# Convolution stages re-ordered behind the FFN's evictions, a fused gate, and rows that are centred but not divided

## The chip, the cores and the metric

The kernel runs on one core of a Trainium2 chip. A core has TensorE (PE; its weight loads are listed apart as PEld), VectorE (DVE), ScalarE (ACT), GpSimd (POOL) and SyncE (SP), each with an in-order queue of its own, and 16 DMA engines that move what the queues of SP, ACT and POOL issue. Times are microseconds (us) on the device. The kernel before took 1149.67 us, the median of 3 runs (1146.87 to 1152.59); the profiled execution took 1154.33.

## The reference

x is 2048 rows of 576, the output has the same shape. Two branches read the normalized rows xn and are added to x:

```python
xn = (x - mean(x)) / sqrt(var(x) + 1e-5)              # per row
# branch A: short causal convolution, product, long convolution, gate
k_shift[s] = sum over t < 4 of k[s - t] * shift_k[:, t]
kv = k_shift * v
y  = irfft(rfft(pad(kv)) * rfft(pad(ssm_k)))[:2048] + kv * ssm_D   # per channel
A  = xn * y
# branch B
B  = relu(xn @ w1) @ w2                                # 576 -> 4608 -> 576
out = x + A + B
```

All is float32. A product is made exact enough by splitting each operand into a rounded high part and the rest (hi, lo) and adding hi*hi, hi*lo and lo*hi.

## The kernel before

**FFN.** The 2048 rows are 16 tiles t of 128 rows, four blocks b of four tiles (BT = 4), two halves of two blocks. For each half, all 12 chunks of 384 hidden units pass over its two blocks. `mm1` (L276) makes one 128x512 block of hidden units in 14 matmuls; ACT's L281 takes relu into hh, DVE's L282 the rest into ll. `mm2` (L296) makes one 128x288 half of an output tile in 9 matmuls; DVE adds it to acc[t] (L299), which began as x. The weights of a chunk are loaded by SP (L234 to L243) and split by ACT (L251, L259) and POOL (L224). `make_xT` computes a block's mean and deviation (`stats`, `inv_std`), normalizes (L181), transposes on PE (L214) and splits into xhi, xlo, xhl. For block 0 this stands at the kernel's start; `make_xT` for the second half is traced in the first half's last chunk.

**Convolution.** The long convolution is a transform of length 2048 with a shift of a quarter bin, so that the product of transforms is the causal convolution's; it is written as 64 x 32, in four stages of a generator `conv`. fk: the table ssm_k (kt, 4.7 MB in packets of 128 bytes, L339) is split (`stack`, L320 on ACT and L321 on DVE) and transformed (`first`, L327) to zk in DRAM. fx: for each tile, the four taps of the short convolution and the product with v (L397 to L405, on DVE), split, transformed to zx. fm, the middle stage, 32 groups: the second step of both transforms (L455), their complex product on ACT and DVE (L471 to L499), the first step back, to zy. fo, the last stage, 16 tiles: the second step back (L537, L539), assembled from PSUM (L541 on ACT, L542 on DVE), gated with the normalized rows (L181, then L549), and added to the FFN's result: for t < 8, whose FFN result was stored to DRAM as fin, on POOL (L553) and stored; for t >= 8 into acc[t] (L556), before the FFN stores it.

**What sets the order.** Every seventh matmul of `mm1` (3,584 columns) and every ninth of `mm2` (2,592 columns) calls `tick` with its columns. A tick credits the convolution `rate` times the columns; when its credit is not negative it runs the generator to the next `yield`. `yield W` costs W of credit; `yield -PAUSE` lets that many FFN columns pass first. That gives the order in which operations are traced. It is not yet the queues' order: a planner (the tile framework's timeline scheduler) then orders each engine's queue by its own estimate of when operands are ready and buffers free, with the traced order as priority. `tc.issue_after(ins)` makes the operations traced within it stand behind `ins` in the queue of ins's engine. How far the planner moves operations shows in the trace: the statistics of the second half's rows (L166 on xn), traced in the twelfth chunk, run at 67 us.

PSUM: two tiles for mm1, three for mm2, three for the convolution and the transposes.

Of the kernel before, what the change touches and what calls it, by code (L numbers as in the profile page):

```python
# [17 lines left out]
P = 128  # L18
# [27 lines left out]
PAUSE = 20000  # L46
START = 40000
PAUSES = 7.5
SHARE = 0.93
# [3 lines left out]
W_FK, W_FX, W_FM, W_FO = 1.6, 4.4, 2.0, 2.8  # L53
KD = 72
# [52 lines left out]
def h3_ffn_kernel(ctx: ExitStack, tc, x, k, v, shift_k, ssm_k, ssm_D, w1, w2, fwd, inv, mid, out):  # L107
# [39 lines left out]
    def move(tile_, rows, t, store=False):  # L147
        for u in range(U):
            a, b = tile_[halves(u)[0]], rows[u, :, t]
            nc.sync.dma_start(*((b, a) if store else (a, b)))  # L150
# [3 lines left out]
    def load_x(t, tag, bufs):  # L154
        pair = xp.tile([P, 2, D], F32, tag=tag, name=f"{tag}{t}", bufs=bufs)
        move(pair, x, slice(t, t + 2))
        return pair

    def load_acc(t):
        pairs[t] = load_x(t, "acc", HT // 2)  # L160
        acc[t], acc[t + 1] = pairs[t][:, 0, :], pairs[t][:, 1, :]
# [21 lines left out]

    xT = {}
    done = {}

    def make_xT(b, srcs, in_place=False):

# [3 lines left out]
        xT[b] = (hi, lo, hl)  # L192
        t0 = b * BT
        with tc.issue_after(done["dve"].ins) if done else nullcontext():
            for t in range(t0, t0 + BT):
                stats(t, srcs[t])
            inv_std(t0, BT)
        xn = []
        for t in range(t0, t0 + BT):
# [6 lines left out]
            normalized(xn[-1], srcs[t], t)  # L206
        for c in range(5):
            w = min(P, D - c * P)
            if b == 0 and c >= 3:
                ps = ps_o.tile([P, 512], F32, tag="o", name=f"psx{c}")  # L210
            else:
                ps = fft_psum()
            for i in range(BT):
                nc.tensor.transpose(ps[:w, i * P:(i + 1) * P], xn[i][:, c * P:c * P + w], ident)  # L214
            if c < 4:
                nc.scalar.activation(hi[:, c, :], ps, AF.Copy)
                nc.vector.tensor_tensor(lo[:, c, :], ps, hi[:, c, :], OP.subtract)  # L217
            else:
                done["act"] = nc.scalar.activation(hl[:64, :], ps[:64, :], AF.Copy)
                done["dve"] = nc.vector.tensor_tensor(hl[64:, :], ps[:64, :], hl[:64, :],  # L220
                                                      OP.subtract)
# [63 lines left out]
    def mm2(ci, b, i):  # L285
        t = b * BT + i
        cols = slice(i * P, (i + 1) * P)
        for h in range(2):
# [10 lines left out]
            nc.vector.tensor_tensor(acc[t][:, dc], ps[:, :NH], acc[t][:, dc], OP.add)  # L299
            tick(W_MM2 / 2)  # L300
        if ci % NCHUNK == NCHUNK - 1:
            if t < HT:
# [26 lines left out]

    def conv():  # L330

        with tc.tile_pool(name="fk", bufs=2) as fp:
            kt = fp.tile([P, NH, A2], F32, tag="kt", name="kt", bufs=1)
            for d in range(0, NH, KD):
# [3 lines left out]
            skip = fp.tile([P, NH], F32, tag="skip", name="skip", bufs=1)  # L340
            for h in range(2):
                nc.sync.dma_start(skip[h * A1:h * A1 + 1, :], ssm_D[None, h * NH:(h + 1) * NH])
            yield -2 * PAUSE
            for h in range(2):
                row = slice(h * A1, h * A1 + 1)
                nc.vector.tensor_tensor(kt[row, :, 0], kt[row, :, 0], skip[row, :], OP.add)

            def prepare(t):
                stk = fp.tile([P, 2, NH], F32R, tag="stk", name=f"ks{t}")
                for h in range(2):  # L350
                    stack(stk[:, h, :], kt[:, :, t], h)
                return stk

            order = [T * u + t for t in range(T) for u in range(U)]
# [4 lines left out]
            nxt = prepare(order[0])  # L359
            yield -PAUSE / 2  # L360
            for n, t2 in enumerate(order):
                stk = nxt
                u, t = divmod(t2, T)
                z = fp.tile([P, D], F32, tag="z", name=f"zk{t2}")
                for h in range(2):
                    first(ws[t], stk[:, h, :], z[:, h * NH:(h + 1) * NH], u)
                    if h == 0 and n + 1 < len(order):
                        nxt = prepare(order[n + 1])
# [6 lines left out]
        with tc.tile_pool(name="fx", bufs=2) as fp:  # L375
# [3 lines left out]
            win = {}  # L379

            def load_k(t):
                win[t] = fp.tile([P, D], F32, tag="k", name=f"k{t}", bufs=KS + 1)
                if t >= 0:
                    move(win[t], k, t)
                else:
# [4 lines left out]
            def prepare(t):  # L390
                if t + 1 < T:
                    load_k(t + 1)
                w = load_const(fp, fwd[t], f"wx{t}")
                vt = fp.tile([P, D], F32, tag="v", name=f"v{t}")
                move(vt, v, t)
                c = fp.tile([P, D], F32, tag="c", name=f"c{t}", bufs=2)
                nc.vector.tensor_tensor(c, win[t], sk[:, 0, :], OP.mult)  # L397
                for n in range(1, KS):
                    e = fp.tile([P, D], F32, tag="e", name=f"e{t}_{n}", bufs=2)
                    nc.vector.tensor_tensor(e, win[t - n], sk[:, n, :], OP.mult)  # L400
                    nc.vector.tensor_tensor(c, c, e, OP.add)  # L401
                return w, vt, c

            def finish(w, vt, c, t):
                nc.vector.tensor_tensor(c, c, vt, OP.mult)  # L405
                stk = fp.tile([P, U, D], F32R, tag="stk", name=f"xs{t}")
                for u in range(U):
                    stack(stk[:, u, :], c, u)
                return w, stk

            for t in range(1 - KS, 1):
                load_k(t)
            pre = prepare(0)
            ready = finish(*pre, 0)
            pre = prepare(1)
            yield -PAUSE
            for t in range(T):
                w, stk = ready
                for u in range(U):
                    z = fp.tile([P, D], F32, tag="z", name=f"zx_{t}_{u}")  # L420
                    for h in range(2):
                        cols = slice(h * NH, (h + 1) * NH)
                        first(w, stk[:, u, cols], z[:, cols], u)
                        if h == 0 and u == 0 and t + 1 < T:
                            ready = finish(*pre, t + 1)
                        yield W_FX
                    nc.sync.dma_start(zx[:, T * u + t, :], z)
                if t + 2 < T:
                    pre = prepare(t + 2)
            yield -PAUSE  # L430


        with tc.tile_pool(name="fm", bufs=2) as fp:
# [6 lines left out]
            def second(z, g, name):  # L440
                zt = fp.tile([P, D], F32, tag="zt", name=f"zt{name}", bufs=3)
                nc.sync.dma_start(zt, rows(z, g))
                hi = fp.tile([P, D], F32R, tag="hi", name=f"hi{name}", bufs=4)
                lo = fp.tile([P, D], F32R, tag="lo", name=f"lo{name}", bufs=4)
                nc.scalar.activation(hi, zt, AF.Copy)
                nc.vector.tensor_tensor(lo, zt, hi, OP.subtract)
                return hi, lo
# [10 lines left out]
            def both(g):  # L458
                return second(zk, g, f"k{g}"), second(zx, g, f"x{g}")

            pend = None
            nxt = both(0)
            yield -PAUSE
            for g in range(NG + 1):
                if g < NG:
                    (kh, kl), (xh, xl) = nxt
                    k1 = fp.tile([P, D], F32, tag="k1", name=f"k1_{g}")
                    k2 = fp.tile([P, D], F32, tag="k2", name=f"k2_{g}")
                    for h in range(2):
                        ps, cols = run(kh, kl, 0, h)  # L470
# [4 lines left out]
                        yield W_FM  # L475
# [202 lines left out]
```

## Time and profile before

| | before |
|---|---|
| median of 3 runs | 1149.67 us (1146.87 to 1152.59) |
| profiled execution | 1154.33 us |
| its span | 1152.5 us |
| mean granted PE clock | 0.977 |
| PE busy | 1095.9 us (95%) |
| DVE, ACT, POOL busy | 707.0, 584.5, 266.4 us |
| moved by DMA | 150.78 MB, 131 GB/s |
| matmuls of fk, fx, fm, fo | 128, 128, 576, 128 of 6534 |

Busy time counts an engine as busy while any of its instructions runs; idle time is put down to what released the engine. The granted clock is the share of PE's full clock; a matmul takes longer where it is below 1. Stretches of the trace are read with PE's busy time and clock side by side, since a wait of PE can be followed by a stretch at a lower clock.

### The profile page before, as it was taken

To read this page: it belongs to the slowest core of one execution; us is meant where nothing else is said; L and a number is where in the kernel's file an instruction comes from. 1 tells how busy PE (TensorE), PEld (TensorE's weight loads), DVE (VectorE), ACT (ScalarE), POOL (GpSimd) and SP (SyncE) were. 2 spreads that over 40 slices of the span, in tenths; PEclk is the share of its full clock that TensorE was granted. 3 is DMA by queue.
4 is the path that set the end of the run, shared out by engine and by line. 5 is a ranking of instruction groups with operands and counts; after the bars stand their busy time and mean duration, and the time that the engine had idled before them with its cause. 6 is when DMAs were issued, how large, how long until landed. Compare 5 with 4: busy or idle time off the path is not lost.

```text
span 1152.5 us, 17373 instructions
## 1 busy us (share of the span) xinstructions
PE 1095.9 (95%) x6534; PEld 990.5 (86%) x6534; DVE 707.0 (61%) x1223; ACT 584.5 (51%) x1178; POOL 266.4 (23%) x207
## 2 busy tenths in 40 slices
PE   7989999899899999999999999999999998886998
PEld 4879899778799899999889899999999997775997
DVE  6367673999976733554665555555555446679832
ACT  3248783344233333566467676666767644344410
POOL 3132313133143123112121220311302213241110
PEclk8989999999999999999999999999999998997999
DMA  9955546465344234333652442333424217676203
GB/s 197 157 142 192 180 148 205 128 192 177 102 146 150 67 115 157 85 95 127 198 165 63 127 128 62 128 96 98 123 65 135 76 33 226 197 223 176 69 1 83
DMA packets 112768, 150.78 MB, mean 131 GB/s; under 512 B 44845, under 2 KB 62895, under 8 KB 112684
## 3 DMA queue, kind: packets, MB, share of 16 engines
q1 hardware_dynamic: 105628, 138.93, 43.2%
q0 software_dynamic: 7056, 10.75, 3.8%
q8 instruction: 51, 0.84, 0.3%
q14 instruction: 33, 0.27, 0.1%
HBM read 114.26 MB, written 35.39 MB: 130 GB/s over the span
## 4 chain that ended last, share of the span: by engine, by line
PE 66%; DVE 11%; DMA 9%; SPq 5%; ACT 4%; issue 3%; POOL 1%; DVEq 0%; ACTq 0%; POOLq 0%
PE pso L296 29%; PE psh L276 29%; PE psf L455 6%; DMA r<-in_w 4%; SPq L339 3%; PE psf L327 2%; DMA xt<-in_x 2%; DVE c L401 2%; DVE e L400 2%; DVE olo L519 1%; DVE acc L299 1%; DMA kt<-in_ssm_k 1%; DVE xs L321 1%; DVE y L542 1%; SPq L234 1%
## 5 line engine op out<-in xcount | busy, mean ns | idle before, releaser
L224 POOL TENSOR_TENSOR l<-r,h 128x640 fp32r<-128x640 f32 (+1 forms) x144 | 227.8, 1596 | 643.3 <-ACT h L259 432.2
L296 PE MATMUL pso<-h,hh 128*128 128x288 f32 x1152 | 340.8, 298 | 12.1 <-DVE acc L299 11.9
L296 PE MATMUL pso<-h,ll 128*128 128x288 f32 x1152 | 340.9, 298 | 4.7 <-DVE ll L282 4.7
L296 PE MATMUL pso<-l,hh 128*128 128x288 f32 x1152 | 340.6, 297 | 0.0
L296 PEld LDWEIGHTS pso<-h,hh 128*128 128x128 f32 x1152 | 218.3, 190 | 21.8 <-DVE acc L299 15.1
L276 PE MATMUL psh<-xhi,h 128*128 128x512 f32 x576 | 228.9, 399 | 4.2 <-DVE ll L282 4.1
L276 PE MATMUL psh<-xlo,h 128*128 128x512 f32 x576 | 228.8, 397 | 0.0
L276 PE MATMUL psh<-xhi,l 128*128 128x512 f32 x576 | 227.9, 396 | 0.0
L296 PEld LDWEIGHTS pso<-l,hh 128*128 128x128 f32 x1152 | 218.7, 190 | 6.0
L296 PEld LDWEIGHTS pso<-h,ll 128*128 128x128 f32 x1152 | 218.5, 190 | 5.5 <-DVE ll L282 5.0
L299 DVE TENSOR_TENSOR acc<-pso,acc 128x288 f32<-128x288 f32 x384 | 169.4, 452 | 78.3 <-PE pso L296 76.1
L282 DVE SCALAR_TENSOR_TENSOR ll<-psh,hh 128x512 fp32r<-128x512 f32 x144 | 98.6, 687 | 130.1 <-ACT hh L281 129.5
L281 ACT ACTIVATE hh<-psh 128x512 fp32r<-128x512 f32 x144 | 85.3, 595 | 159.1 <-PE psh L276 131.1
L276 PEld LDWEIGHTS psh<-xhi,h 128*128 128x128 f32 x576 | 109.6, 191 | 22.9 <-DVE ll L282 5.7
L276 PEld LDWEIGHTS psh<-xhi,l 128*128 128x128 f32 x576 | 109.9, 191 | 20.8
L276 PEld LDWEIGHTS psh<-xlo,h 128*128 128x128 f32 x576 | 109.9, 191 | 16.7 <-DVE xlo L217 0.2
L251 ACT ACTIVATE h<-r 128x640 fp32r<-128x640 f32 x72 | 52.4, 736 | 74.7 <-DMA r<-in_w 46.9
L492 DVE TENSOR_TENSOR k<-psf,k 128x288 f32<-128x288 f32 x64 | 29.2, 456 | 74.3 <-ACT sw L491 66.8
L259 ACT ACTIVATE h<-r 128x576 fp32r<-128x576 f32 x72 | 46.6, 680 | 53.1 <-DMA r<-in_w 39.2
L490 ACT ACTIVATE sw<-psf 64x288 f32<-64x288 f32 x64 | 26.2, 409 | 67.5 <-PE psf L455 66.8
L276 PE MATMUL psh<-xhl,h 128*128 128x512 f32 x144 | 56.8, 395 | 1.1 <-DVE xhl L220 1.1
L321 DVE TENSOR_TENSOR ks<-kt,ks 64x288 fp32r<-64x288 f32 x64 | 46.6, 731 | 16.9 <-ACT ks L320 15.1
(100 smaller groups left out, 1417.3 us busy)
## 6 DMA issues: line engine op xcount, KB each, us to landing
r<-in_w SPq DMA_DIRECT2D x24, 864.0 KB, 4.9
r<-in_w SPq DMA_DIRECT2D x23, 768.0 KB, 6.0
zk<-zk SPq DMA_DIRECT2D x32, 288.0 KB, 2.5
zx<-zx SPq DMA_DIRECT2D x32, 288.0 KB, 3.2
ztk<-zk SPq DMA_DIRECT2D x32, 288.0 KB, 2.8
ztx<-zx SPq DMA_DIRECT2D x32, 288.0 KB, 2.8
zy<-vo SPq DMA_DIRECT2D x32, 288.0 KB, 2.1
zo<-zy SPq DMA_DIRECT2D x16, 576.0 KB, 6.1
```

The source lines that it names most:

```text
L224: return nc.gpsimd.tensor_tensor(dst, src, hi, OP.subtract)
L251: nc.scalar.activation(h1, r1[:, :, cols], AF.Copy)
L259: nc.scalar.activation(h2, r2[:, j, :], AF.Copy)
L276: nc.tensor.matmul(ps, a, m, start=i == 0, stop=i == len(seq) - 1)
L281: done["act"] = nc.scalar.activation(hh, ps, AF.Relu)
L282: nc.vector.scalar_tensor_tensor(ll, ps, 0.0, hh, op0=OP.max, op1=OP.subtract)
L296: nc.tensor.matmul(ps[:, :NH], a[:, cols], m[:, dc], start=n == 0, stop=n == 3 * FT - 1)
L299: nc.vector.tensor_tensor(acc[t][:, dc], ps[:, :NH], acc[t][:, dc], OP.add)
L321: nc.vector.tensor_tensor(dst[other], src[own], dst[own], OP.subtract)
L339: nc.sync.dma_start(kt[halves(h)[0], d:d + KD, :], src)
L455: nc.tensor.matmul(ps[:, :NH], a, m[:, cols], start=n == 0, stop=n == 2)
L492: nc.vector.tensor_tensor(k1[:, cols], ps, k1[:, cols], OP.mult)
```

## The change

Three things change.

**Order of the convolution.** `here()` puts an operation of the convolution on DVE behind the FFN's last traced addition (`done["acc"]`) and one on ACT behind the last traced relu (`done["act"]`). In every stage the loads, the splits and the arithmetic are taken apart and traced in small pieces between yields, loads first: kt in 16 pieces with a pause after each; x rows, matrices and z one to three steps ahead of their use, with more buffers; the short convolution tap by tap, two tiles ahead. The constants of the pacing change with it.

**Rows.** `make_xT` subtracts the mean only (`centred`). As relu and both products are homogeneous in a row's scale, 1/deviation is applied where the second product's sum is added to acc (`scalar_tensor_tensor`, same line count on DVE). `first_xT` is a new path for block 0: each tile is centred as its mean is ready, by ACT (even tiles, with the negative mean as bias) or DVE (odd), and transposed; the deviations follow. Its x rows are loaded through the queues of SP and ACT, ahead of the warm-up's other work.

**Gate.** L181, L549 and L553 or L556 become two fused DVE operations: (x - mean) * y, then that * 1/deviation + the FFN's result. The finished tiles t < 8 are stored through POOL's queue. `rest_of_stream` runs out the convolution before the last chunk's rows t >= 8 are stored.

```diff
-PAUSE = 20000
-START = 40000
-PAUSES = 7.5
-SHARE = 0.93
+PAUSE = 16000
+START = 4000
+PAUSES = 16
+SHARE = 0.95
...
-W_FK, W_FX, W_FM, W_FO = 1.6, 4.4, 2.0, 2.8
-KD = 72
+W_FK, W_FX, W_FM, W_FO = 1.6, 3.7, 1.8, 2.1
+KD = 36
+KT_GAP = 6000
...
+    def centred(dst, src, t):
+        return nc.vector.tensor_scalar(dst, src, mv[:, t, 0:1], None, op0=OP.subtract)
...
+    def first_xT(srcs):
...
+        for t in range(BT):
...
+            with tc.issue_after(behind.ins) if behind else nullcontext():
+                stats(t, srcs[t])
+                if t % 2 == 0:
+                    behind = nc.vector.tensor_scalar(neg[:, t:t + 1], mv[:, t, 0:1], -1.0, None,
+                                                     op0=OP.mult)
+                    nc.scalar.activation(xn, srcs[t], AF.Identity, bias=neg[:, t:t + 1])
+                else:
+                    behind = centred(xn, srcs[t], t)
+            for c in range(5):
+                w = min(P, D - c * P)
+                nc.tensor.transpose(ps[c][:w, t * P:(t + 1) * P], xn[:, c * P:c * P + w], ident)
+        for c in range(5):
+            split_x(0, c, ps[c])
+        with tc.issue_after(done["dve"].ins):
+            inv_std(0, BT)
...
-            normalized(xn[-1], srcs[t], t)
+            centred(xn[-1], srcs[t], t)
...
-            nc.vector.tensor_tensor(acc[t][:, dc], ps[:, :NH], acc[t][:, dc], OP.add)
+            done["acc"] = nc.vector.scalar_tensor_tensor(
+                acc[t][:, dc], ps[:, :NH], rstd[:, t:t + 1], acc[t][:, dc],
+                op0=OP.mult, op1=OP.add)
...
+            if t >= HT:
+                rest_of_stream()
...
+    @contextmanager
+    def here():
+        with tc.issue_after(done["acc"].ins), tc.issue_after(done["act"].ins):
+            yield
...
+                    yield -KT_GAP
...
-            yield -2 * PAUSE
+            yield -PAUSE
             for h in range(2):
                 row = slice(h * A1, h * A1 + 1)
-                nc.vector.tensor_tensor(kt[row, :, 0], kt[row, :, 0], skip[row, :], OP.add)
+                with here():
+                    nc.vector.tensor_tensor(kt[row, :, 0], kt[row, :, 0], skip[row, :], OP.add)
...
+            def tap(t, n):
...
+                with here():
...
+                        e = fp.tile([P, D], F32, tag="e", name=f"e{t}_{n}", bufs=1)
+                        nc.vector.tensor_tensor(e, win[t - n], sk[:, n, :], OP.mult)
+                        nc.vector.tensor_tensor(sums[t], sums[t], e, OP.add)
...
+                side = (((gate, t + 1),), ((split, t + 1, 0),),
+                        ((split, t + 1, 1),), ((tap, t + 2, 0),),
+                        ((tap, t + 2, 1),), (),
+                        ((tap, t + 2, 2),), ((tap, t + 2, 3),))
...
+                        for part in range(2):
+                            for what, *args in side[4 * u + 2 * h + part]:
+                                what(*args)
+                            yield W_FX / 2
...
+            def gate(t):
+                if t >= 0:
+                    with here():
+                        nc.vector.scalar_tensor_tensor(ys[t], rest[t][1], mv[:, t, 0:1], ys[t],
+                                                       op0=OP.subtract, op1=OP.mult)
+            def add(t):
+                if t >= 0:
+                    to, more = (ys[t], rest[t][2]) if t < HT else (acc[t], acc[t])
+                    with here():
+                        nc.vector.scalar_tensor_tensor(to, ys[t], rstd[:, t:t + 1], more,
+                                                       op0=OP.mult, op1=OP.add)
+                    if t < HT:
+                        move(to, out, t, store=True, queues=(nc.gpsimd, nc.gpsimd))
...
+                    if h == 0:
+                        if n + 1 < len(units):
+                            split(*units[n + 1])
+                        if n + 3 < len(units):
+                            load_z(*units[n + 3])
+                    else:
+                        (gate if u == 0 else add)(t - 1)
+                        if u == 0:
+                            load_rest(t + 2)
+                    yield W_FO
...
+    for t in range(0, BT, 2):
+        load_acc(t, queues=(nc.sync, nc.scalar))
+    load_w1(0)
+    load_w2(0)
...
-    make_xT(0, acc)
+    first_xT(acc)
```

In fm the diff does the same with `load` and `split` per tensor, two groups ahead, and moves the sum of the complex product and its split (L495, L498, L499) into the next group's first two steps.

More of the change, by code (lines that the diff above doesn't have):

```diff
@@ L648, in h3_ffn_kernel @@
     drain(BT)
-    for _ in stream:
-        pass
+    rest_of_stream()
 def kernel(**inputs):
```

343 lines of the change are left out of this document (187 added, 156 removed).

## The prediction

> **What bounds the kernel now.** First the page's busy times and the core's clock:
>
> ```profile
> PE 1095.9 (95%) x6534; PEld 990.5 (86%) x6534; DVE 707.0 (61%) x1223; ACT 584.5 (51%) x1178; POOL 266.4 (23%) x207
> ```
>
> ```profile
> core 0: 1152.5 us, clock 0.977
> ```
>
> TensorE bounds it: no other engine is busy for more than 61%. But 5% is not all that can be won. Busy time at the granted clock is 1095.9 x 0.977 = 1070.7 us of full-speed work, so 1152.5 - 1070.7 = 81.8 us go to waits and to the slow clock after them. The matmuls stay the same in number, so this is the most that the change can win. The view by stretches shows where it lies (columns: stretch, width, busy time of PE, weight loads, DVE, ACT, POOL, then clock, DMA share, GB/s):
>
> ```profile
> 0.00:20.00 20.00, 12.97 (x44) 7.00 (x44) 10.73 (x25) 5.16 (x9) 5.49 (x9) 0.84 0.99 228
> 50.00:70.00 20.00, 15.28 (x67) 12.81 (x66) 8.76 (x20) 5.51 (x9) 3.16 (x2) 0.83 1.18 206
> 185.00:217.00 32.00, 29.44 (x166) 26.47 (x165) 17.61 (x31) 5.73 (x10) 4.26 (x4) 0.95 0.55 152
> 217.00:300.00 83.00, 75.32 (x432) 66.43 (x432) 82.25 (x113) 32.15 (x62) 25.37 (x18) 0.98 0.54 162
> 300.00:390.00 90.00, 87.41 (x532) 79.45 (x531) 72.64 (x110) 31.34 (x60) 24.55 (x18) 1.00 0.44 132
> 545.00:605.00 60.00, 56.56 (x353) 51.71 (x353) 39.69 (x79) 34.97 (x75) 11.51 (x8) 0.97 0.62 178
> 945.00:1065.00 120.00, 99.57 (x520) 85.52 (x520) 85.03 (x144) 52.85 (x105) 37.50 (x34) 0.89 0.69 200
> 1020.00:1050.00 30.00, 21.15 (x95) 16.75 (x94) 25.61 (x42) 15.54 (x32) 13.29 (x11) 0.85 0.79 225
> 245.40:248.00 2.60, 0.36 (x3) 0.03 (x1) 2.57 (x4) 0.00 (x0) 2.05 (x2) 1.00 0.52 176
> 249.00:252.50 3.50, 3.50 (x16) 3.40 (x16) 3.47 (x7) 1.01 (x2) 0.00 (x0) 0.52 0.07 21
> ```
>
> Width less PE busy x clock is the loss of a row: 9.1 us at the start, 7.3 around 60 us, 4.0 + 9.2 + 2.6 = 15.8 in the x transform (fx), 5.1 where the second half's rows come in, 31.4 in the last stage (fo). That is 68.7 of the 81.8; the rest is thin, or the tail.
>
> What such a loss is made of stands in the chain of waits (start, length, what), then in DVE's and PE's timelines around 60 us:
>
> ```profile
> 49.10 11.44 DMA kt<-in_ssm_k
> 63.91 5.27 PE psh L276 x14
> 69.18 2.38 PE pso L296 x18
> 71.56 3.20 PE psh L276 x14
> ```
>
> ```profile
> 49.81 0.46 DVE L299 TENSOR_TENSOR acc<-pso,acc 128x288 f32<-128x288 f32 x1 [0.36 <-PE pso L296]
> 60.65 1.40 DVE L346 TENSOR_TENSOR kt<-kt,skip 1x288 f32<-1x288 f32 x2 [10.38 <-DMA kt<-in_ssm_k]
> 62.08 0.69 DVE L282 SCALAR_TENSOR_TENSOR ll<-psh,hh 128x512 fp32r<-128x512 f32 x1
> ```
>
> ```profile
> 62.82 0.61 PE L296 MATMUL pso<-h,ll 128*128 128x288 f32 x1 [4.72 <-DVE ll L282]
> ```
>
> The convolution's addition L346 stands at the head of DVE's queue until its load lands at 60.5; the FFN's own L282 is queued behind it, and PE waits for L282. Then 14 matmuls take 5.27 us where 3.20 is the full-speed price: the wait is paid twice. In fo the view of waits shows the same figure (total us, times, longest), and DVE's timeline at fx's entrance too:
>
> ```profile
> DVE xt L181 <- DMA xt<-in_x: 22.2, 10, 4.4
> PEld psf L537 <- DVE y L542: 21.6, 23, 2.8
> ```
>
> ```profile
> 203.03 0.76 DVE L400 TENSOR_TENSOR e<-k-1_1956,sk 128x576 f32<-128x576 f32 x1 [9.72 <-DMA k-1_1956<-in_k]
> ```
>
> L181 waits for x rows, the evictions L542 stand behind it, and PE waits for the PSUM they free. What costs PE is DVE's in-order queue with load-fed operations too early in it.
>
> **The slow clock.** The last two stretches above are a wait and what follows it: some 2.2 us without a matmul, then 3.5 us at clock 0.52, 1.7 us more. [...]
>
> **The start.** Rows of the timelines of DVE, PE and ACT:
>
> ```profile
> 8.54 1.54 DVE L166 BATCH_NORM_STATS2 bn<-acc 128x6 f32<-128x288 f32 x4 [0.73 <-DMA acc<-in_x]
> ...
> 12.59 4.32 DVE L181 TENSOR_SCALAR xn<-acc,mv,rstd 128x576 f32<-128x576 f32 x4
> ```
>
> ```profile
> 14.37 0.87 PE L214 MATMUL psf<-ident,xn 128*128 128x128 f32 x3 [5.52 <-DVE xn L181]
> ...
> 19.28 1.22 PE L276 MATMUL psh<-xhi,h 128*128 128x512 f32 x2
> ```
>
> ```profile
> 18.63 1.57 ACT L216 ACTIVATE xhi<-psf 128x512 fp32r<-128x512 f32 x3 [5.72 <-PE psf L214]
> ```
>
> Now the statistics of all four tiles and the whole deviation chain (to 12.59) precede the first centring. The change centres a tile as soon as its mean is there, two tiles on DVE and two on ACT, transposes tile by tile, and puts the deviation behind. The last rows still land near 8.5: the DMA share is 0.99, so a second issuing queue moves them little. From there: statistics of two tiles, 1.9 us; one centring, 1.1 (4.32 / 4); five transposes of 0.29, 1.5; one copy to xhi, 0.6. That is 13.6 against 19.28, a little earlier where DVE and ACT overlap, a us later where ACT must first split weights. I take a gain of **6** (3 to 7).
>
> **The kernel's table (kt).** Eight loads become 16 halves, and by the count of ticks L346 moves to about 200,000 of the FFN's columns, some 90 us of its work (0.45 ns a column, from 3.20 us for 7,168 and 2.38 for 5,184), where the same bytes, landed at 60.5 now, are long there. Gone: the wait of 4.7 and about 2.8 of slow clock. Kept as risk: the same bytes still pass through SP's queue ahead of the second chunk's w2, which the FFN now wants 6 us sooner. Gain **6** (2 to 7.5).
>
> **The x transform.** Groups by line on DVE (busy us, mean ns, idle before), then the tile c (ns: least, median, most):
>
> ```profile
> L299 DVE TENSOR_TENSOR acc<-pso,acc 128x288 f32<-128x288 f32 x384 | 169.4, 452 | 78.3 <-PE pso L296 76.1
> L282 DVE SCALAR_TENSOR_TENSOR ll<-psh,hh 128x512 fp32r<-128x512 f32 x144 | 98.6, 687 | 130.1 <-ACT hh L281 129.5
> L321 DVE TENSOR_TENSOR ks<-kt,ks 64x288 fp32r<-64x288 f32 x64 | 46.6, 731 | 16.9 <-ACT ks L320 15.1
> L401 DVE TENSOR_TENSOR c<-c,e 128x576 f32<-128x576 f32 x48 | 44.1, 922 | 0.3
> ```
>
> ```profile
> L401 DVE TENSOR_TENSOR c<-c,e x48: 740/751/2402, 207.0 to 393.0; 128x576 f32<-128x576 f32 x48
> ```
>
> DVE's work is the same: per t eight products and sums at 0.92 and two splits at 0.73, 8.8 us. What changes is place. Each tap goes behind the FFN's last traced evictions, about one per tick, and 16,000 columns (7.2 us) lie between loads and first tap, so most of the 9.7 us wait goes. Counting ticks by the new constants (819.2 of price over 0.95 x 2,027,520 - 256,000 - 4,000 columns is 1.48 credited per mean tick of 3,017 columns, and what the pauses saved up is spent here), a t lasts 25,300 columns: 11.45 us of FFN and 8 matmuls of 0.13, 12.5 us. In it DVE has 8.8 + 4.8 x 0.452 + 1.8 x 0.687 = 12.2 by mean durations, which count the overlap of neighbours twice: near 90%, at most 98. The stage becomes orderly but not loose. From 217 to 300, with DVE 99% full, PE lost 11%; from 300 to 390, 81% full, 3%. Between these over 200 us, 6 to 22 us; I take 9, nearer the looser row, against 15.8: gain **7** (-6 to 10).
>
> **The last stage.** Its rows on the tile xt:
>
> ```profile
> L181 DVE TENSOR_SCALAR xt<-xt,mv,rstd x16: 564/580/1625, 957.6 to 1083.2; 128x576 f32<-128x576 f32 x16
> L549 DVE TENSOR_TENSOR y<-y,xt x16: 740/742/1144, 976.7 to 1089.9; 128x576 f32<-128x576 f32 x16
> ```
>
> Removed per t: L181 and its load wait, L549, and L556 on DVE or an addition on POOL. Added: two fused operations. The trace has no such operation on SBUF alone; 0.58 and 0.74 bound each, and I take 0.74, the two-tensor one, so 1.5 for 1.3 to 2.1: no work is won. The order is: nothing load-fed stands at DVE's head before a load issued two t earlier, z comes in halves three units ahead, and the stores leave SP's queue for POOL's. The pace is 16,400 columns and 8 matmuls a t, 8.5 us. In the first eight t each needs 288 KB of two z, x, fin and out and 128 KB of matrix, 1.57 MB per 8.5 us, beside weights of 1.8 MB per 43 us: 227 GB/s, where 1020 to 1050 us moves 225 at a share of 0.79. It fits with little spare. Of 31.4 I leave 6 (3 to 17): gain **25.5** (14 to 28).
>
> **At nothing.** 1/deviation in the second product's sum: the fused form with PSUM input takes 0.687 for 512 columns (L282), which between proportion and an unchanged price makes 0.39 to 0.69 for 288, against 0.452: -25 to +92 us on DVE over 384. I take 0.46, since 0.75 for 576 and 0.452 for 288 show a small fixed part. It hides under the matmuls except in fx, where the upper end is rival 1. The middle stages, whose losses are thin, and the second half's rows (5.1), whose statistics wait as before, stay.
>
> **Sum.** 6 + 6 + 7 + 25.5 = 44.5. The profiled execution took 1154.33, so 1109.8; it lies 4.7 above the median of the runs shown, so **1105** on the median's scale.
>
> **Rivals.** (1) *fx is DVE-bound.* DVE's and POOL's timelines near 970 us:
>
> ```profile
> 969.20 5.17 DVE L519 TENSOR_TENSOR olo<-zo,ohi 128x576 fp32r<-128x576 f32 x1 [0.66 <-ACT ohi L518]
> ```
>
> ```profile
> 969.39 4.36 POOL L224 TENSOR_TENSOR l<-r,h 128x576 fp32r<-128x576 f32 x3
> ```
>
> A DVE operation with two SBUF inputs, 0.75 in the median, takes 2 to 5 us beside POOL's weight splits: L519 sits out three of them. Taps, gate and final addition are of that kind and stand between the FFN's evictions. If PE loses 11% over 200 us, fx costs 22 instead of 9: 1118. [...] (2) *The last stage stays dense.* If the convolution lags its pacing, its 16 t crowd before the end, transfers come late to the gate, and about two thirds of 31.4 stay, 20 rather than 6: 1119. Against it: the middle stage's loads now run two groups ahead. (3) *The planner undoes it.* Pauses order the program, not the engines; if fx's and fo's waits only move, start and kt alone remain: 1154.3 - 12 - 4.7 = 1138. (4) *Slower: PE takes the waits.* Splits now stand behind FFN evictions, and 384 groups of convolution matmuls (64 + 64 + 192 + 64) stand in PE's in-order queue. If each finds its split late by 0.2 us, less than half an L299 ahead of it, that is 77 us: 1182; from 0.12 us on (44.5 / 384) the change loses. For it: a nearly full DVE in fx. Against: a tick or more of FFN lies between split and use.
>
> **How the numbers follow.** Forecast 0.50, (1) 0.20, (2) 0.14, (3) 0.09, (4) 0.07. About 0.5% (6 us) is what a measurement of this kernel tells from no change; the first three are faster by more, (3) may shrink to nothing: faster 0.88, same 0.04, slower 0.08. The good ends (7 + 7.5 + 10 + 28) give 1097, and 1080 if the second half's rows and the thin losses go too; the high end is (3). Range 1080 to 1138.
>
> **What would show it.** First L276 matmul near 13.5 us; no wait of PE above 2 us near 60; L346 and the gate without a DMA wait; DVE near 90% in fx at clock 0.99 or more; fo with clock above 0.97. Wrong: many waits of PE for DVE splits, clock below 0.95 in fx, or matmuls of fo after the FFN's last chunk.

## The result, and the profile after

The changed kernel takes 1118.33 us (median of 4 runs, 1114.96 to 1124.28) where the kernel before takes 1150.61: a ratio of 0.973 with an interval of 0.968 to 0.978. It is 32 us faster. The forecast was 1105, 45 us faster; the sign and the range held, and 13 us of the expected gain did not come. The profiled execution took 1114.96.

The page's busy times and the core's clock, after:

```profile
PE 1080.5 (97%) x6534; PEld 980.5 (88%) x6534; DVE 737.3 (66%) x1215; ACT 583.5 (52%) x1180; POOL 265.4 (24%) x215
```

```profile
core 0: 1113.2 us, clock 0.989
```

Full-speed work is 1080.5 x 0.989 = 1068.6 us, as before; so 44.6 us are lost now instead of 81.8. The same view by stretches as in the prediction (stretch, width, busy time of PE, weight loads, DVE, ACT, POOL, clock, DMA share, GB/s) says where:

```profile
0.00:20.00 20.00, 16.72 (x62) 9.74 (x63) 12.53 (x30) 9.35 (x16) 9.02 (x12) 0.91 0.95 227
20.00:60.00 40.00, 38.81 (x226) 34.34 (x225) 16.91 (x45) 10.43 (x19) 9.42 (x8) 1.00 1.03 199
60.00:120.00 60.00, 57.60 (x341) 51.93 (x340) 28.12 (x56) 15.00 (x25) 17.89 (x12) 1.00 0.26 80
225.00:258.00 33.00, 32.45 (x193) 29.14 (x193) 22.82 (x35) 8.28 (x14) 9.40 (x7) 1.00 0.68 201
258.00:350.00 92.00, 89.64 (x543) 81.17 (x542) 87.70 (x119) 35.23 (x69) 26.71 (x21) 1.00 0.50 151
350.00:462.00 112.00, 109.71 (x669) 100.00 (x668) 94.74 (x135) 40.76 (x79) 26.94 (x21) 1.00 0.41 130
510.00:560.00 50.00, 50.00 (x320) 46.19 (x319) 31.14 (x67) 31.11 (x67) 7.02 (x5) 1.00 0.64 191
980.00:1090.00 110.00, 94.86 (x522) 82.99 (x521) 96.92 (x163) 54.12 (x112) 23.34 (x34) 0.91 0.66 194
```

The x transform (225 to 462 us) runs at full clock and loses 5.2 us, with DVE 95% and then 85% full. The stretch in which the second half's rows come in (510 to 560) loses nothing. The last stage, at clock 0.91, loses 110 - 94.86 x 0.91 = 23.7 us: more than half of what is left.

For the runs below the loss is also counted from PE's matmuls alone: for each, the time to the next one's start less the full-speed price, summed over the stretch between a stage's first and last matmul. The stage's borders are its own matmuls, so a row does not add up to the loss of the stretches above. The prices are read at clock 1.00: 0.229 us for 512 columns and 0.132 for 288 (before, 14 in 3.20 us from 71.56 and 18 in 2.38 from 69.18), 0.110 for a transpose (after, eight from 23.20 in 1.04 us, the last of which takes 0.27: 0.77 / 7). In us:

| kernel | time | start and kt | fk and entrance of fx | fx | fm | fo | longest run in fo |
|---|---|---|---|---|---|---|---|
| before | 1150.6 | 21.1 | 5.7 | 15.4 | 8.3 | 36.0 | 20 |
| after | 1118.3 | 11.7 | 1.5 | 6.2 | 1.7 | 25.5 | 44 |
| fm_price | 1097.8 | 13.6 | 2.4 | 5.9 | 0.4 | 9.6 | 10 |
| psum_four | 1111.2 | 14.2 | 9.8 | 9.9 | 3.5 | 2.4 | 6 |
| early | 1112.7 | 11.8 | 5.1 | 3.7 | 1.9 | 22.5 | 26 |
| no_here | 1118.0 | 11.4 | 2.0 | 13.8 | 2.8 | 20.2 | 28 |
| old_start | 1121.0 | 13.6 | 3.2 | 6.5 | 2.4 | 25.7 | 44 |
| plain_sum | 1111.5 | 13.1 | 0.4 | 5.0 | 5.4 | 17.4 | 20 |
| old_gate | 1124.7 | 12.4 | 2.1 | 5.7 | 3.1 | 33.3 | 42 |
| fm_plain | 1090.4 | 10.5 | 0.5 | 5.6 | 1.1 | 4.3 | 4 |
| late_plain | 1100.0 | 12.2 | 2.2 | 6.3 | 1.5 | 7.9 | 8 |
| kt_now | 1119.8 | 13.4 | 1.2 | 7.7 | 5.7 | 23.6 | 26 |
| even | 1098.3 | 12.9 | 5.2 | 2.6 | 5.2 | 4.5 | 4 |
| wide_fx | 1093.4 | 14.7 | 4.4 | 3.2 | 2.7 | 2.9 | 5 |

The last column is the longest run of convolution matmuls in PE's order without a matmul of the FFN between them. Start and kt varies between 10.5 and 14.7 among kernels whose first rows are prepared by the same text, so a stage's difference of up to 4 us in one profile shows nothing by itself.

The longest waits of PE and the one convolution load that DVE still waits for (total us, times, longest):

```profile
PEld psf L657 <- DVE y L660: 19.8, 18, 1.7
PE psf L657 <- DVE y L660: 14.9, 14, 1.5
PE pso L334 <- DVE acc L337: 7.6, 7, 2.4
DVE e L457 <- DMA k-1_2411<-in_k: 4.7, 1, 4.7
```

The waits of DVE for kt and for xt are gone. What PE waits for in fo is unchanged in name: the PSUM that the eviction L660 (L542 before) frees. But nothing stands in front of that eviction for a load any more. PE's and DVE's timelines of after, and the stretch around them, show what does it now:

```profile
1043.55 0.61 PE L657 MATMUL psf<-ohi,wi 128*128 128x288 f32 x1 [1.16 <-DVE y L660]
...
1045.79 0.61 PE L657 MATMUL psf<-ohi,wi 128*128 128x288 f32 x1 [0.91 <-DVE y L660]
...
1048.30 0.61 PE L657 MATMUL psf<-ohi,wi 128*128 128x288 f32 x1 [1.17 <-DVE y L660]
1048.70 0.44 PE L658 MATMUL psf<-olo,wi 128*128 128x288 f32 x1
1048.94 0.51 PE L334 MATMUL pso<-h,hh 128*128 128x288 f32 x1
```

```profile
1045.30 0.93 DVE L660 TENSOR_TENSOR y<-psf,low 64x288 f32<-64x288 f32 x2
1046.26 0.82 DVE L632 SCALAR_TENSOR_TENSOR acc<-y,rstd,acc 128x576 f32<-128x576 f32 x1
1047.00 0.75 DVE L618 TENSOR_TENSOR olo<-zo,ohi 128x576 fp32r<-128x576 f32 x1
1047.78 0.46 DVE L660 TENSOR_TENSOR y<-psf,low 64x288 f32<-64x288 f32 x1
1048.27 0.94 DVE L337 SCALAR_TENSOR_TENSOR acc<-pso,rstd,acc 128x288 f32<-128x288 f32 x2
```

```profile
1025.00:1048.00 23.00, 12.65 (x45) 9.04 (x43) 21.14 (x38) 14.80 (x32) 7.15 (x13) 0.64 0.89 264
1025.00:1031.20 6.20, 3.30 (x17) 2.13 (x15) 4.82 (x10) 5.02 (x11) 2.19 (x4) 1.00 0.85 267
1031.20:1048.00 16.80, 9.35 (x28) 6.91 (x28) 16.33 (x29) 9.79 (x22) 4.96 (x9) 0.50 0.91 263
```

From 1025.3 to 1048.9 us PE does nothing but 44 matmuls of the convolution, from the seventh on four at a time, each group behind a split, two evictions and one of the gate's two operations on DVE, which is 92% busy. No matmul of the FFN stands between them. The granted clock is 1.00 in the first 6 us of it and 0.50 in the rest; 0.64 is the mean. The run ends less than two us after the first addition of the convolution to an acc tile, L632, is done (1047.1); L337, the FFN's addition, follows it on DVE. In the traced order the FFN's additions to acc[t], t >= 8, come after the convolution's addition to the same tile; so once the convolution lags, the FFN cannot go on until it has caught up. That reason for the block is argued from the order; the run itself is shown.

### The profile page after: what moved, and what is told of

It reads as the page before. It is cut to its first block, busy times and chain, and to the rows that moved or that the text cites. A ratio compares the mean times of both kernels' runs of the same rounds, so it can differ in the third digit from the quotient of the medians.

```text
span 1113.2 us, 17349 instructions
## 1 busy us (share of the span) xinstructions
PE 1080.5 (97%) x6534; PEld 980.5 (88%) x6534; DVE 737.3 (66%) x1215; ACT 583.5 (52%) x1180; POOL 265.4 (24%) x215
## 4 chain that ended last, share of the span: by engine, by line
PE 69%; DVE 16%; DMA 6%; issue 4%; ACT 3%; SPq 1%; POOL 1%; DVEq 0%; ACTq 0%; POOLq 0%
PE pso L334 30%; PE psh L314 29%; PE psf L533 6%; DVE e L457 4%; DVE acc L337 3%; DVE c L458 3%; DMA r<-in_w 2%; PE psf L369 2%; DVE ll L320 1%; DVE xs L363 1%; DVE c L454 1%; SPq L392 1%; DVE c L463 1%; DMA k-1_2411<-in_k 1%; POOL l L262 1%
## 5 line engine op out<-in xcount | busy, mean ns | idle before, releaser
L337 DVE SCALAR_TENSOR_TENSOR acc<-pso,rstd,acc 128x288 f32<-128x288 f32 x384 | 193.4, 512 | 90.1 <-PE pso L334 88.3
L334 PEld LDWEIGHTS pso<-h,hh 128*128 128x128 f32 x1152 | 216.3, 188 | 17.4 <-DVE acc L337 11.3
L314 PE MATMUL psh<-xlo,h 128*128 128x512 f32 x576 | 226.2, 393 | 0.0
L314 PE MATMUL psh<-xhi,l 128*128 128x512 f32 x576 | 225.6, 392 | 0.0
L297 ACT ACTIVATE h<-r 128x576 fp32r<-128x576 f32 x72 | 46.9, 678 | 52.7 <-DMA r<-in_w 29.1
L314 PE MATMUL psh<-xhl,l 128*128 128x512 f32 x144 | 56.5, 392 | 0.0
```

The costliest lines, as they stand in the source:

```text
L297: nc.scalar.activation(h2, r2[:, j, :], AF.Copy)
L314: nc.tensor.matmul(ps, a, m, start=i == 0, stop=i == len(seq) - 1)
L334: nc.tensor.matmul(ps[:, :NH], a[:, cols], m[:, dc], start=n == 0, stop=n == 3 * FT - 1)
L337: done["acc"] = nc.vector.scalar_tensor_tensor(acc[t][:, dc], ps[:, :NH], rstd[:, t:t + 1], acc[t][:, dc], op0=OP.mult, op1=OP.add)
```

## The experiments

**Why the last stage is dense: fm_price, psum_four, early.** Theory A: the middle stage lags its pacing, the last one starts late and crowds. Along PE's order of matmuls fm ends at 0.901 of the FFN's columns and fo starts at 0.911, while the pacing traces fm's end at 0.804. Three edits, each alone, move that:

```diff
 fm_price
-W_FK, W_FX, W_FM, W_FO = 1.6, 3.7, 1.8, 2.1
+W_FK, W_FX, W_FM, W_FO = 1.6, 3.7, 2.4, 2.1
 psum_four
-    ps_o = ... bufs=3        ps_f = ... bufs=3
+    ps_o = ... bufs=2        ps_f = ... bufs=4
 early
-KT_GAP = 6000
+KT_GAP = 2000
```

> One number changes: a step of the middle stage is priced 2.4 instead of 1.8 credits, so that its steps are traced at about the pace at which they stand in PE's queue, and the last stage's additions into acc are traced later. Theory A (the last stage is dense because the convolution lags its traced order by about 10% of the FFN, and the FFN's own additions into acc[t] must wait for the convolution's addition to the same tile, traced before them): no stretch of fo without FFN matmuls, fo's loss falls from 23.7 us to 8 to 12, median 1104 (1099 to 1109). Rival B (fo costs PE because DVE and the transfers are nearly full over its 16 tiles, wherever they stand): fo still loses about 20, median 1114 to 1119.

> Four PSUM tiles for the convolution instead of three, two for the FFN's second product instead of three. Theory A with its cause (the middle stage lags because three PSUM tiles let only three of its six products per group stand in PE's queue at a time): fm ends near 0.81 of the FFN's columns instead of 0.90, fo spreads over 13% of them, no stretch without FFN matmuls, fo's loss below 10. Against it works the FFN's own wait for PSUM: each of 384 sums has one tile less ahead; if a tenth of them waits 0.3 us, 12 us. Median 1106 (1098 to 1116). Rival B: fo's loss stays near 20 and the FFN's wait comes on top, 1125 or more.

> The pause between pieces of kt is 2,000 columns instead of 6,000, so that every stage is traced and stands about 35 us earlier. Theory A: the lag is one against the traced order, and the order moves along, so fo is still crowded before the first addition into acc (a stretch of some 26 matmuls instead of 44 without FFN between): loss of fo 15 to 20, median 1113 (1109 to 1118). Rival C (fo is simply too late against the FFN's end): fo gets 35 us more room, its loss falls below 10, median 1104.

fm_price took 1097.84 us (ratio 0.953, 0.950 to 0.956), 20 us less than the change for one constant and a us below theory A's range: fo starts at 0.882 and its loss falls from 25.5 to 9.6. psum_four took 1111.19 (0.966, 0.962 to 0.969): fo starts at 0.820 and loses 2.4, but 12 us more than in the change are lost from fk to fx. early took 1112.74 (0.967, 0.964 to 0.969), inside theory A's range; its run is 26 as forecast, but fo still loses 22.5, more than the 15 to 20 that theory A gave. The stage's stretch in the first two, then three of psum_four's waits:

```profile
958.00:1070.00 112.00, 106.68 (x632) 96.19 (x631) 100.59 (x169) 57.45 (x116) 33.03 (x39) 0.98 0.69 200
```

```profile
916.00:1057.00 141.00, 139.84 (x850) 127.59 (x850) 110.29 (x193) 61.33 (x126) 43.27 (x46) 1.00 0.57 170
```

```profile
PE pso L334 <- ACT h L297: 6.5, 3, 3.0
PE pso L334 <- DVE acc L337: 5.4, 8, 1.6
PE psf L369 <- DVE xs L363: 3.9, 5, 1.5
```

Theory A holds in the main. In fm_price's fo DVE is 90% busy (89% in the change, from 983 to 1084 us), the core moves 200 GB/s (202), and PE still has a clock of 0.98 (0.90): DVE's load and the transfers over the whole stage do not decide, its crowding does. The run without FFN matmuls is a part of that. By the same count some 18 of the change's 25.5 us are lost in the run of 44, but only some 12 of early's 22.5 in its run of 26; most of the rest is lost within some 15 us of the run. The room that fo has, from its first to its last matmul in the FFN's columns, orders the kernels made from the change almost as well: 0.064 in the change, 0.079 in early, 0.085 in plain_sum, 0.092 in fm_price, and 0.099 to 0.132 in the five that lose less than 8. No run here tells room and run apart. That psum_four moves fm's end to 0.805, almost where it is traced, shows that the convolution's three PSUM tiles are what holds fm back. What the exchange costs elsewhere is not the sums' PSUM: PE's waits for it are shorter than in the change (5.4 for 7.6). PE waits instead for a split of weights on ACT (L297) and for the x transform's splits on DVE (L363); why these come later is not shown.

**Is it the order or the pauses? no_here.** The convolution's operations lose their place behind the FFN's evictions; pauses, pieces and early loads stay.

```diff
     def here():
-        with tc.issue_after(done["acc"].ins), tc.issue_after(done["act"].ins):
-            yield
+        yield
```

> Nothing is ordered behind the FFN's last traced eviction any more; pauses, pieces and buffers stay. Theory D (the ordering is what removes the waits at kt and fx): waits of 3 to 10 us of DVE on loads return near 60 and 230 us, PE loses 8 to 15 us more, median 1126 to 1133. Rival E (the pauses and the loads taken apart do it alone): median within 4 us of 1118.

It took 1117.96 (0.971, 0.968 to 0.974), no different from the change in total; theory D falls. The waits it named stay away as well: the planner moves the addition to kt up to 53.8 us, where it waits 0.2 us for its load, and the tap at fx's entrance waits 4.0 us (4.7 in the change). By stage it isn't nothing: fx loses 13.8 instead of 6.2 (PE's waits for the FFN's sum grow from 7.6 to 10.6 us in all), and fo, whose run is 28, loses 5 less. So rival E has the total by a balance of two stages. The place in the queue seems worth some 7 us in fx, by one profile of each; that the pauses and the early loads do the rest is not shown, since no run leaves them out there.

**The parts: old_start, old_gate, kt_now.**

```diff
 old_start
-    first_xT(acc)
+    make_xT(0, acc)
...
 old_gate
-   nc.vector.scalar_tensor_tensor(ys[t], rest[t][1], mv[:, t, 0:1], ys[t], subtract, mult)
+   normalized(rest[t][1], rest[t][1], t)
+   nc.vector.tensor_tensor(ys[t], ys[t], rest[t][1], OP.mult)
-   nc.vector.scalar_tensor_tensor(to, ys[t], rstd[:, t:t + 1], more, mult, add)
+   nc.vector.tensor_tensor(to, ys[t], more, OP.add)
 kt_now
-KT_GAP = 6000
+KT_GAP = 1
-            yield -PAUSE        (between kt's loads and the addition to kt)
```

> The changed kernel with block 0's rows prepared in the old order (all four tiles' statistics, the deviations, then centring and transposes together), the rest as changed; the computation is whole. Theory S, the start's gain is real and nothing takes it back: the first FFN matmul moves from 13.8 us to 17.5 to 19.5, and the time rises by as much, from 1118.3 to 1122 to 1125. Rival T, the start is hidden, since the second chunk's weights or the kernel's table set the pace after it: first FFN matmul later by the same, but the time within 2 us of 1118.3.

> The changed kernel with the gate in three DVE operations (centre and divide, product, sum) at the same places in the order as the two fused ones; the computation is whole. Theory H, no work is won by the fusion where it counts: 16 operations of 0.58 us more, partly beside waits of PE, so 1116 to 1122. Rival I, DVE sets the last stage's end, each operation more shows there in full: 1126 to 1129.

> The changed kernel with the 16 loads of the table traced one after the other without pauses, and the addition to the table traced right behind them (still behind the FFN's last addition); the computation is whole. The kernel with pauses of 2000 took 1112.7 and loses 11.8 us ahead of the first fk matmul; this one's longest run of convolution matmuls in the last stage is the same, 26. Theory M, the wait at the table's addition was the loss around 60 us and the pause is what removes it: DVE waits 4 us or more for the table, PE behind it with a slow clock after, 16 to 20 us lost ahead of fk, 1116 to 1121. Rival N, being behind the FFN's last addition in the queue is enough, or the loads alone land in time: no such wait, 1109 to 1114.

old_start took 1120.99 (0.974, 0.972 to 0.976), 2.7 us more than the change. PE's timeline at the start of after:

```profile
13.78 1.01 PE L314 MATMUL psh<-xhi,h 128*128 128x512 f32 x2 [0.32 <-ACT xhi L202]
14.59 0.71 PE L314 MATMUL psh<-xlo,h 128*128 128x512 f32 x1
...
17.58 0.39 PE L314 MATMUL psh<-xhi,l 128*128 128x512 f32 x1
...
22.30 0.40 PE L334 MATMUL pso<-h,hh 128*128 128x288 f32 x1 [0.23 <-ACT hh L319]
```

and of old_start:

```profile
17.60 1.22 PE L315 MATMUL psh<-xhi,h 128*128 128x512 f32 x2
...
25.33 0.40 PE L335 MATMUL pso<-h,hh 128*128 128x288 f32 x1 [0.23 <-ACT hh L320]
```

The first matmul is 3.8 us later, the first of the second product 3.0, the median 2.7. Started at 13.78, PE has a clock of 0.54 to 17.5, 0.43 us from one matmul to the next instead of 0.23; started at 17.60, its matmuls stand 0.43 us apart only to 19.4: that gives a part back. The total lies a us below theory S's range and a us above rival T's, and the change's own runs spread over 9 us, so the total doesn't decide. The trace does at the start: 3.0 us of the gain are still there at the second product.

old_gate took 1124.68 (0.978, 0.975 to 0.981), 6.4 more than the change: between the two expectations, nearer to I. Sixteen times the three operations' means less the two's, (0.780 + 0.746 + 0.830 - 0.886 - 0.887) x 16 = 9.3 us of DVE work, and fo's loss grows by 7.8. But the work is not all that this edit brings back. L182, the centring and division, waits for x rows at DVE's head again, which the fused L625 does nowhere; the view of waits, then one of its operations and the wait of PE behind it:

```profile
DVE xt L182 <- DMA xt<-in_x: 6.3, 8, 1.9
```

```profile
1007.53 3.83 DVE L182 TENSOR_SCALAR xt<-xt,mv,rstd 128x576 f32<-128x576 f32 x1 [0.96 <-DMA xt<-in_x]
```

```profile
1011.91 0.41 PE L656 MATMUL psf<-ohi,wi 128*128 128x288 f32 x1 [2.43 <-DVE y L659]
```

So theory H's total falls, and how much of the 6.4 us is DVE's work and how much these waits is not separated.

kt_now took 1119.78 (0.969, 0.965 to 0.974). That is M's number, but not its place. DVE's timeline has the table's addition at 73.73 without any wait for its load:

```profile
73.30 0.52 DVE L337 SCALAR_TENSOR_TENSOR acc<-pso,rstd,acc 128x288 f32<-128x288 f32 x1 [1.00 <-PE pso L334]
73.73 1.61 DVE L401 TENSOR_TENSOR kt<-kt,skip 1x288 f32<-1x288 f32 x1
```

The stretch ahead of fk loses only 1.6 more than in early. So for that wait the place in the queue is enough, as N said. Of the rest of the 7.0 us to early, fx has 4.0, fm 3.8 and fo 1.1, with 3.9 less at fx's entrance. Neither theory has these. For fm the timelines of DVE and PE show what came between, and the stretch what it cost:

```profile
541.46 1.54 DVE L167 BATCH_NORM_STATS2 bn<-xn 128x6 f32<-128x288 f32 x4 [6.00 <-DMA xn<-in_x]
```

```profile
549.11 0.61 PE L532 MATMUL psf<-hik,m_sb 128*128 128x288 f32 x1 [1.86 <-DVE k L584]
```

```profile
545.00:555.00 10.00, 7.74 (x37) 6.56 (x36) 8.79 (x24) 6.53 (x15) 0.00 (x0) 0.83 0.58 177
```

The statistics of the second half's last rows stand at DVE's head for 6.00 us until the rows land (0.90 in early, 2.22 in the change, 5.91 in the kernel before). PE then waits 1.86 us for L584, an eviction behind them on DVE, the clock of the stretch is 0.83, and 10 - 7.74 x 0.83 = 3.6 us go. That is the kind of wait which the change removes from the convolution and leaves in the FFN. Why fx loses more stays open.

**1/deviation in the sum: plain_sum, fm_plain, late_plain.**

```diff
-            centred(xn[-1], srcs[t], t)
+            normalized(xn[-1], srcs[t], t)
-            done["acc"] = nc.vector.scalar_tensor_tensor(...)
+            if b == 0:
+                done["acc"] = nc.vector.scalar_tensor_tensor(...)
+            else:
+                done["acc"] = nc.vector.tensor_tensor(acc[t][:, dc], ps[:, :NH], acc[t][:, dc], OP.add)
 fm_plain: the same, and W_FM = 2.4;  late_plain: fm_plain with  b < 2  in place of  b == 0
```

> The changed kernel with the rows of blocks 1 to 3 divided by their deviation when they are centred, and their second product added with the plain two-tensor sum; only block 0 keeps 1/deviation in the sum. The computation is whole. By the trace of the changed kernel the sum with the factor takes 0.512 us against 0.452 without, so 288 sums are 17 us less work on DVE. Theory F, DVE's load costs where it is nearly full: fx loses 3 to 5 us instead of 6.2, and fo, whose longest run of convolution matmuls without the FFN's is 20 in this kernel's queue order instead of 44, loses 15 to 20 instead of 25.5: 1107 to 1112. Rival G, the dearer sum is hidden under the matmuls and the run's length does not count: 1116 to 1120.

> The kernel with the middle stage's price at 2.4, which took 1097.8, and in it the plain sum for blocks 1 to 3. With the last stage no longer dense, theory F (DVE's load costs in fx and fo) gives 3 to 6 us: 1092 to 1095. Rival G (the dearer sum is hidden) gives 1096 to 1100. No run of ten or more convolution matmuls without the FFN's stands in its queue order, as in the kernel it is made from.

> The kernel that took 1090.4 us (middle stage's price 2.4, rows of blocks 1 to 3 divided when centred, plain sums), with block 1 as the change has it: only blocks 2 and 3, whose sums run beside the middle and the last stage, keep the plain sum. The computation is whole. The kernel with 1/deviation in all sums and the same price took 1097.8. Theory J, the dearer sum costs in the last stage, beside an almost full DVE: fo loses 4 to 5 us as in the kernel of 1090.4, and the time is 1089 to 1092. Rival K, it costs in the x transform and the table's stage, which run beside blocks 0 and 1: 1095 to 1099, with fo's loss near 4.3 all the same. Rival L, by count of operations, half of the gain goes: 1093 to 1095.

The groups of DVE in after, and in plain_sum, which has both forms (busy us, mean ns, idle before):

```profile
L337 DVE SCALAR_TENSOR_TENSOR acc<-pso,rstd,acc 128x288 f32<-128x288 f32 x384 | 193.4, 512 | 90.1 <-PE pso L334 88.3
```

```profile
L342 DVE TENSOR_TENSOR acc<-pso,acc 128x288 f32<-128x288 f32 x288 | 127.2, 450 | 65.9 <-PE pso L334 64.6
L338 DVE SCALAR_TENSOR_TENSOR acc<-pso,rstd,acc 128x288 f32<-128x288 f32 x96 | 48.4, 511 | 21.1 <-PE pso L334 20.2
```

The factor costs 0.061 us a sum, 384 x 0.061 = 23 us of DVE. plain_sum took 1111.53 (0.965, 0.964 to 0.967), 6.8 less than the change, and fm_plain **1090.41** (0.947, 0.945 to 0.949), 7.4 less than fm_price: about the same gain twice, in the first pair inside theory F's range and in the second a little more than it. It beats the change by 28 us. But where it comes from isn't settled. late_plain took 1099.97 (0.953, 0.949 to 0.957), no better than fm_price, so J falls: the plain sum of blocks 2 and 3, which run beside fo, brings nothing; L falls with it. K comes within a us of the total, but not of the place: fo loses 7.9 in late_plain and 4.3 in fm_plain, though both have the same sums there, and the rest of the difference is spread thinly. Between these two the edit to block 1 decides the total; that the work saved does it is not shown, since with each of these edits the order of the matmuls moves as well: the longest run in fo is 10 in fm_price, 8 in late_plain and 4 in fm_plain, and 44 and 20 in the change and plain_sum.

**Is there more? even, wide_fx.** Both are fm_plain with KT_GAP 2000, PAUSES 12 and prices 2.3 and 2.6 for fm and fo; SHARE 0.97 in the first, 0.98 and a price of 4.6 for fx in the second.

> The kernel that took 1090.4 us with other pacing: the table's pauses 2000 instead of 6000, prices 2.3 and 2.6 for the middle and the last stage, so that the last stage runs from 0.838 to 0.965 of the FFN's columns instead of 0.873 to 0.975 and has a quarter more room. The computation is whole. Theory A (density of the last stage makes its loss) gives fo 1 to 3 us instead of 4.3: 1086 to 1089. Rival: what is left in fo is not density, or the earlier fk and fx lose as much: 1090 to 1095.

> The kernel with the even pacing and the x transform's price at 4.6 instead of 3.7, a share of 0.98: in the queue order fx has some 0.02 of the columns more to run in, and the last stage starts at 0.862. The computation is whole. If what is left in fx (5.6 us) comes of DVE being nearly full there, fx loses 2 to 4 us, while fo keeps 2 to 4: 1084 to 1088. Rival: fx's short waits come one by one from operations beside weight splits, whatever the width: fx stays at 5 to 6, 1088 to 1092.

even took 1098.32 (0.951, 0.948 to 0.954), wide_fx 1093.37 (0.947, 0.944 to 0.951), each above both of its expectations. fo in even loses as much as in fm_plain, and it loses some 5 at fx's entrance and 5 in fm: the rival's case, and worse. wide_fx has fx at 3.2 as expected, but even has 2.6 without the wider price, so the width isn't shown to be the cause. fm_plain stays the best; its stretch of fo:

```profile
945.00:1060.00 115.00, 112.77 (x679) 102.95 (x678) 99.51 (x173) 57.41 (x116) 30.98 (x39) 0.99 0.66 193
```

## Why the prediction was right, and where it was not

The frame held: PE bounds, the matmul work is the same (1070.7 and 1068.6 us), and the gain is what waits and the slow clock gave up. That the total came as near as it did is in part luck: one term fell short by 15 us, and gains that the sum had not counted made up for most of it. By the count from the matmuls the profiled executions differ by 39.5 us: start and kt 9.4, fx with fk and its entrance 13.4, fm 6.6, fo 10.5, and -0.4 behind it.

- **The start** (6): the first FFN matmul came at 13.78, predicted near 13.5, 5.5 us earlier than before. In the time it is worth less, 4.4 us by the first matmul of the second product (26.69 before, 22.30 now): started earlier, PE does more of its first work at a low clock (0.54 from 13.78 to 17.5 us; before, 0.84 from 19.28 to 22.8), which the sum left out.
- **kt** (6): the wait at the addition is gone, and PE's wait of 4.72 us near 60 with it. The sign "no wait of PE above 2 us near 60" fails by a little: one of 2.40 remains at 70.0, for an L337 queued on DVE behind the statistics and the centring of block 2's rows. With the start it makes 9.4 where 12 stood. kt_now shows that the addition's new place in DVE's queue is enough to keep the wait away, and in no_here it stays away without that place.
- **fx** (7, leaving 9): better than said, 6.2 left, 13.4 gained with what lies ahead of it. The wait of 9.7 us for k shrank to 4.7 (L457). DVE near 90% at clock 1.00 came as described (89% from 258 to 462 us); rival 1, the bound by DVE (1118), is not what happened, though the total lies beside its price. no_here puts the order's part at some 7 us.
- **The second half's rows** ("stay"): wrong, they lose nothing now, and fm's loss fell by 6.6 in all. The statistics still wait for rows on DVE (7.2 us in all, 6.2 before), but in this stretch for 2.22 us instead of 5.91, and PE waits nowhere. In kt_now the same wait is 6.00 and some 3.6 us go again, so this gain hangs on when the rows land; nothing in the change was meant to bring it.
- **fo** (25.5, leaving 6): this is the term that failed. 10.5 came (7.7 by the stretches, 31.4 to 23.7). The step was "nothing load-fed stands at DVE's head": true, L625 and L632 have no wait for a load. But the pace "16,400 columns and 8 matmuls a t" took the traced order for the order of the matmuls: PE's order has 16 t in 0.064 of the columns, 8,100 a t. With three PSUM tiles fm ran on to 0.90 of the columns, fo started late, and 44 convolution matmuls stood in a row; fm_price and psum_four move the start of fo and take most of the loss away. That is rival 2's condition at rival 2's time, 1119. Its second half is wrong: the transfers are not late to the gate, the chain of splits, evictions and gates on DVE is too long (DVE 92% busy in the run of 44). ACT's splits do wait for z five times, 11.5 us in all, but all before 993 us, ahead of the run.
- **1/deviation** (0.46 for 0.452, hidden): 0.512, inside the bounds 0.39 to 0.69. "It hides under the matmuls" is in doubt: two pairs of runs gain 7 us without it, though late_plain, with the factor in half of the sums, keeps none of that.
- **The fused gate** (no work won): right in direction, DVE has no less work, as eight additions for t < 8 were POOL's; but the two operations took 0.886 and 0.887 us in the mean, above the 0.58 to 0.74 that were to bound them. Three operations at the same place cost 6.4 us more, by work and by waits for x rows (old_gate).
- **Rival 3**: no_here has the changed kernel's total without the order, but start and kt are not all that is left. **Rival 4**: no wait of PE for a split of the convolution is among the waits above a microsecond; it didn't happen.

The sum: of 44.5, fo fell short by 15.0 and start and kt by 2.6; fx gave 6.4 more with what lies ahead of it and fm 6.6, and 0.4 was lost behind fo. That is 5.0 short by the count, 5.2 by the profiled executions (1114.96 for 1109.8). The other 8 us to the forecast are the executions profiled: the forecast took off 4.7 for the one before, and the one after lay 3.4 below its median. Against the median of 1150.61 above, the 4.7 is 3.7.

## What to carry to other kernels

Where work is paced into another stream, read from the trace where each stage's matmuls really stand, not where they are traced: here the middle stage, held up by three PSUM tiles, ended at 0.901 of the columns (0.805 with four), and the last one crowded behind it. Look for long runs of one stream on the bounding engine; here one constant that broke up a run of 44 took 20 us off. When load-fed operations are moved off the head of a queue, look for those that stay there: the rows' statistics cost nothing in one order and 3.6 us in the next. A factor moved into another operation is free only by measurement: here it adds 60 ns to each of 384 sums, and two pairs of runs were 7 us faster without it, by a way that is not shown.

## What was not expected of the hardware

- The fused sum with a factor per partition, on PSUM and SBUF, took 511 ns for 128x288 where the plain sum took 450, in one kernel. On SBUF alone the fused gate took 0.82 us for 128x576 (L632) where the split L618 took 0.75.
- From 1025 to 1048 us no wait of PE was longer than 1.3 us, with waits of 0.8 to 1.3 us one every 1.8 to 2.5 us; still the granted clock was 0.50 from 1031.2 to the end of the stretch. The next matmul follows an L658 after 0.24 us (1048.70 to 1048.94), where the full-speed price is 0.13.
